# Sliding-window attention and token mixing on one core: heads on the two partition halves, products in quarter tiles, nine-token loads

## The chip, the core and the metric

The kernel runs on one core of a Trainium2 chip. The core has five engines with queues of their own: PE (TensorE) multiplies matrices and writes to the accumulators in PSUM (eight banks), DVE (VectorE) and ACT (ScalarE) read PSUM and write SBUF, POOL (GpSimd) here mostly issues the loads that turn float32 into float16 on the way, and SP (SyncE) issues the stores. Both memories have 128 partitions. The metric is device time in microseconds (us), lower is better.

## The reference

Eight batches of eight heads, 576 tokens, 64 features a head. Attention has a causal window of 128 tokens and a bias that falls with distance; its output, 512 features a token, goes through a token-mixing layer without a softmax. Inputs and output are float32. Cut to what matters:

```python
def _attn_ref(q, k, v):                      # (8, 8, 576, 64) each
    scores = scale * np.matmul(q, k.transpose(0, 1, 3, 2))
    rel = pos[:, None] - pos[None, :]
    slopes = 2.0 ** (-8.0 * (np.arange(H) + 1) / H)
    bias = slopes[:, None, None] * (-np.abs(rel))[None]
    mask = (rel >= 0) & (rel < 128)
    scores = np.where(mask, scores + bias[None], -1000000000.0)
    attn = softmax(scores)
    return np.matmul(attn, v)

def _moe_ref(x, w_q, w_k, w_out):            # x: (8, 576, 512)
    wq, wk = x @ w_q, x @ w_k                # (8, 576, 64)
    W_tok = scale * np.einsum('bsd,btd->bst', wq, wk)
    mixed = np.einsum('bst,btd->bsd', W_tok, x)
    return np.maximum(mixed, 0.0) @ w_out
```

## The kernel before

Everything is written out as some 770 small operations ("ops": one group of matmuls, one copy, one load). They are numbered as they are made, and the text `ORDER` lists them in the order in which they are emitted: the number, a letter for the engine (P, A, D, G for POOL, S for SP), for PE the PSUM bank, and sometimes `+n/b`, which puts n matmuls of zeros (`keep`, line 592) ahead of the op. Each engine works through its own ops strictly in this order and waits where one needs another's result. A few copies may go to ACT or DVE; `ORDER` says to which.

A batch goes through these steps. The names are those of the ops.

- Loads (line 239, on POOL): for batches 1 to 5 the first 512 tokens of q and k come in rows of two tokens (`ldqk`), the last 64 apart (`ldqkt`); batches 6 and 7 (`ONE`) come in rows of one token; batch 0 comes in rows of six tokens (`ldsix`), into the buffer that later takes outputs. v comes in rows of one token, one transfer for every 128 tokens (`ldv`).
- Transposes on PE through the identity matrix (`tsix` line 339, `tqk` lines 360 and 366, `tqkt` line 382), and copies out of PSUM by ACT or DVE (lines 220 and 222), which put q and k with features on the partitions: two heads on 128 partitions.
- Scores (`sc`, line 415): ten matmuls for a pair of heads and half of its keys. Each uses a quarter of PE's array, 64 rows by 64 columns; keys are on the partitions of the result. ACT takes the exponential (`exp`, line 420), 768 elements a partition in one instruction.
- Mask and bias as a table of factors `bt` (made at lines 251 to 268). For every pair of heads DVE multiplies twice: `edge` (line 435, 512 elements) writes the part of the window that crosses into the next block of 128 keys to a place of its own, and `mul` (line 439, 1,536 elements) treats the rest in place.
- Values (`pv`, line 459): 18 matmuls for a pair of heads, on the whole array (128 keys by 128 queries as weights), 65 columns each: 64 features and a column of ones that gives the softmax's sum. DVE takes the reciprocal (`rec`, line 472) and scales (`nrm`, line 475).
- Transposes of the result (`xt`, line 491) with a copy (`ext`), then the mixing: `wqk` (508), `wkt` (526), `g` (538), `mx` (554) with relu (`emx`, 561 and 563), and the output product `po` (575): four matmuls of 512 columns, a copy (`eo`), and a store (`st`, 582).

PE's matmuls come in five shapes (rows by columns of the array): 128x128 (`pv`, `xt`, `wqk`, `wkt`, `po`, `tqkt`, `tqk` of `ONE`, the zeros), 64x64 (`sc`), 128x64 (`tqk`, `g`), 64x128 (`mx`) and 96x64 (`tsix`). Going through `ORDER`, the shape changes 151 times. There are 2,362 matmuls, each with a weight load of its own, 43 of them of zeros.

Of the kernel before, what the change touches and what calls it, by code (L numbers as in the profile page):

```python
# [7 lines left out]
FP32 = mybir.dt.float32  # L8
F16 = mybir.dt.float16
# [4 lines left out]
P = 128  # L14
S = 576
# [11 lines left out]
0D 1D 32G 2G 28G 3D 22D 31G 4D 30G 29G 33G 137G 23D 6A 9A 53P7+13/7 35G 7A 11A 45P6 34G 134G 51P5+4/0 136G 52A  # L27
49P4 21G 50D 47P5+3/0 46D 133G 72P0 48A 74P2 55P4 132G 8A 5A 54A 40G 63P5+3/6 75A 59P7 39G 60D 12A 73A 36G 13D
61P2+3/2 16D 76D 43G 57P1+1/7 62A 56D 149P7 17G 64A 38G 147P0 85P2 58A 65D 135G 148D 18A 94P4 86A 150D 145P6
44G 95A 96P2+1/0 146D 83P0 97A 143P5+1/7 37G 10A 77D 42G 144A 14D 41G 78P2+1/4 84A 98D 228G 79D 186P6+3/4 80D  # L30
26G 87D 164P4+2/0 19D 99D 25G 151P3+1/0 165A 142G 66D 100P0 15A 152A 138G 88D 67P4 187A 188P2 139G 101D 68D
102D 189A 89P6 140G 69D 175P0 81P3 176A 141G 90D 166P4 91D 103P2 229G 104A 82D 92P7+2/0 190D 177P0 167A 153P2
232G 191D 178A 70P6+1/6 227G 24D 240P5+2/4 168D 71A 93D 231G 154A 179D 105P6+1/0 180D 321G 20A 241A 155P0 169D
230G 106A 107A 320G 108P5+1/2 170P2 109A 192P6 322G 156A 193D 244P5 194D 324G 110P4 181P0 171D 319G 172D 111A
245A 112P6 416G 182D 157D 114P2 238P4 115A 158D 242P5 323G 113A 118P2 239A 119D 159P6 234G 243D 195P3 160D
183D 270P4 246P2 235G 161D 116P0 247A 117D 173P7 336P6 419G 174D 271A 272P0 337D 184P2 273A 338P7 418G 196A
274D 248P0 250P4 237G 275D 332P6 249A 251A 339D 283P0 233G 162P3 281P4 163A 252D 333D 185A 236G 282A 334P7
197P2 27G 253D 284A 259P4 329G 335A 198D 330P6 260A 414G 285D 200P7 431P1 199A 201D 261P4 325G 331D 432A 202P7
417G 262A 203D 353P0 340P2 286D 415G 210P6 354A 351P4 211D 352A 326G 254P0 263D 341A 276P6 255D 327G 256D
364P4 362P2 264D 363A 287P0 365A 328G 277D 129P3 288D 278D 342P4 511G 289D 130A 375P6 257P2 343A 265P0 510G  # L40
126P3 344D 376A 258D 601G 429P5 345D 290P4 127A 208P6 291A 266D 433P3 507G 267D 209A 425P2 355D 279P4 434A
366D 268P7 509G 373P0 280D 430A 269D 204P3 426D 374A 516G 206P6 427P5 207A 292P0 605G 356D 428A 346P6 508G
205D 293A 123P5 347D 294A 506G 348D 295P4 448P2 377D 296A 705G 435P0 124D 449A 297P7 421G 436A 459P4 298D
357P2 367D 424G 460A 301P0 457P6 302A 358D 368P4 359D 458A 602G 446P0 369D 468P2 447A 370D 521P7 422G 349P6
469A 378D 305P0 470P4 423G 471A 212P3 461D 350D 306A 522D 437P4 420G 472D 299P6 303P0 438A 519P2 304D 213A
523P5 439D 706G 520A 517P4 462D 379P0 610G 518A 300D 120P3 606G 380D 524A 221P2 381D 697G 121D 371P7 222A
616P6 698G 450D 372A 382P5 617D 527P0 383A 609G 360P4 451D 538P2 361A 525P7 604G 440D 528A 384P4 514G 539A
526D 560P0 385A 607G 452P2 386D 387P7 215P6 561A 603G 453D 388A 562P4 454D 608G 216A 529P0 389P7 563A 473D
699G 716P6 530A 441P2 564D 512G 540P4 717D 551P0 390D 620P6 513G 442D 552A 224P7 621D 565D 541A 515G 463P0
225A 443D 391P4 700G 549P6 464D 392D 622P3 550A 702G 444P2 623D 618P5 445A 703G 397P6 465D 393P3 624P2 398A  # L50
619D 704G 395P0 394A 712P7 531D 396A 626P5 701G 625D 637P3 627A 474P0 532D 615G 307P2 638A 475D 713D 639P5
613G 308A 476D 714P4 640A 614G 533P2 715D 650P0 612G 542D 628P6 310P5 534D 629A 553D 543D 611G 466P4 651A
720P7 707G 535D 311A 218P6 709G 721A 630D 648P0 641D 544P2 631D 711G 649A 718P7 545D 219A 708G 566P0 546D 719A
455P5 567D 313P6 710G 467D 456A 568D 733P2 735P4 554D 632P0 736A 316P7 633D 314A 634D 555P4 734A 724P0 317A
556D 722P2 477P6 557D 725A 318S 217S 125S 399P7 131S 128S 220S 478D 723A 744P0 642D 661P4 659P2 745A 411P6
652D 737D 400A 726D 405P1 660A 653D 401S 547P7 662A 727D 643P2 412A 569P0 548D 406A 479P4 413S 226S 644D 570A
645D 536P7 480D 558P6 408P3 559D 481A 482P2 537D 755P0 409D 483A 746P4 757P6 756A 663D 410S 571P2 214S 315S
664D 747A 484P1 758A 572D 665P4 485D 573A 748D 574P7 646P6 666D 575A 488P0 667D 490P2 489A 576P7 486P4 491A
728P0 577D 487A 647D 492P2 582P6 729D 635P5 730D 583A 494P4 493A 759D 578P0 636D 584P6 580P2 760D 579A 497P5
581A 738D 654P0 585A 761P2 495A 655D 656D 739P6 498A 496S 223S 122S 309S 407S 500P4 749D 731P5 740D 668P1 762D  # L60
741D 732A 402P0 669D 750P6 763D 742P5 403A 657P1 751D 752D 586P3 404S 312S 658A 764P2 743A 753P7 765D 670P0
754D 587D 766P6 671D 589P5 672D 767A 673P3 769P2 590D 503P1 674D 592P5 501D 504A 770D 675P3 768A 505S 499S
502S 588S 591S 771P4 676A 593A 677P0 683P2 772D 595P7 678A 594S 684D 775P4 773P0 596D 679P2 598P6 776A 680D
597S 774A 681P4 779P2 599A 777P0 685P7 682D 778A 600S 780D 694P6 686A 784P5 687S 695D 691P4 696S 785D 790P7
786S 692D 793P6 693S 791D 688P5 792S 794D 787P4 795S 689A 781P7 690S 788D 789S 782A 783S
# [4 lines left out]
class Op:  # L70
    def __init__(self, name, engs, emit):
        self.name, self.engs, self.emit = name, engs, emit
        self.deps, self.ps_new, self.ps_read = set(), [], []
        self.eng = None
        self.pad = self.padbank = 0
# [11 lines left out]
class Plan:  # L87
# [5 lines left out]
    def op(self, name, engs, emit, reads=(), writes=(), ps_new=(), ps_read=()):  # L93
        o = Op(name, engs, emit)
# [21 lines left out]
    def run(self):  # L116
# [20 lines left out]
        assert len(order) == len(self.ops)  # L137
        return order


BOTH = ("ACT", "DVE")
FILL = ("ACT", "DVE", "POOL")
# [3 lines left out]
NPT = 6  # L146
# [5 lines left out]
ONE = (6, 7)  # L152
PTW = 64 + 4 * 256

VW = 80


@with_exitstack
def kernel(
# [16 lines left out]
    wone = pool.tile([P, P], F16, name="wone")  # L176
    rel = pool.tile([P, 256], I32, name="rel")
    wm = pool.tile([P, 256], FP32, name="wm")
    wtmp = pool.tile([P, 256], FP32, name="wtmp")

    bt = pool.tile([P, H, 512], F16, name="bt")
# [3 lines left out]
    nat = [[pool.tile([P, 2, 2 * DM], F16, name=f"nat{x}{i}") for i in range(NN)] for x in "qk"]  # L185
    ntl = [pool.tile([P, DM], F16, name=f"ntl{i}") for i in range(NN)]
    vn = [pool.tile([P, NT, H, VW], F16, name=f"vn{i}") for i in range(NV)]
    qkT = [pool.tile([P, 2, 4, S], F16, name=f"qkT{i}") for i in range(NQ)]


    pts = [pool.tile([P, 2, PTW], F16, name=f"pt{i}") for i in range(NPT)]
    inv = [pool.tile([P, 2, NT], FP32, name=f"inv{i}") for i in range(4)]
    xs = [pool.tile([P, NT, DM], F16, name=f"x{i}") for i in range(NX)]
# [10 lines left out]
    osh = osa.bitcast(F16)  # L204
    six = [osh[0:96, NOS - 6 + 3 * x : NOS - 3 + 3 * x].rearrange("p a n -> p (a n)").rearrange("p (h e) -> p h e", h=H)
           for x in range(2)]
# [17 lines left out]
    def fill(e, o, x):  # L224
        if e == "POOL":
            nc.gpsimd.memset(o, float(x))
        elif e == "DVE":
            nc.vector.memset(o, float(x))
        else:
            n = 1  # L230
            for y in o.shape[1:]:
                n *= y
            w = (wone if x else wz)[o.base_partition() : o.base_partition() + o.shape[0], 0:n]
            names = "abc"[: len(o.shape) - 1]
            k = dict(zip(names, o.shape[1:]))
            nc.scalar.copy(o, w.rearrange(f"t ({' '.join(names)}) -> t {' '.join(names)}", **k))
# [3 lines left out]

    def setup():
        plan.op("zero", ("DVE",), lambda e: nc.vector.memset(wz, 0.0), writes=["wz"])  # L242
        plan.op("one", ("DVE",), lambda e: nc.vector.memset(wone, 1.0), writes=["wone"])
        plan.op("iota", ("POOL",),
                lambda e: nc.gpsimd.iota(rel, pattern=[[1, 256]], base=0, channel_multiplier=-1),
                writes=["rel"])
        plan.op("idn", ("DVE",),
                lambda e: nc.vector.tensor_scalar(out=idn, in0=rel[:, 0:128], scalar1=0, scalar2=None,
                                                  op0=ALU.is_equal), reads=["rel"], writes=["idn"])
# [388 lines left out]
```

## Time and profile before

| | us |
|---|---|
| median of 3 runs | 148.21 |
| lowest and highest run | 147.70, 148.61 |
| span of the profiled execution, first to last instruction | 146.2 |
| PE busy in the span | 134.8 |
| DVE busy | 122.2 |
| ACT busy | 109.6 |
| POOL busy | 86.1 |

The span leaves out what lies before the first and after the last instruction. The profiled execution's whole time isn't listed apart; the median is 2.0 us above its span. The profile's page gives busy times, the span in 40 slices, the DMA queues and the chain of work that ended last. Its other views are groups of instructions by line and shape ("busy, mean ns of one | idle before"), a table by stages, a timeline in order of time, and the chain piece by piece. A busy PE isn't PE at its peak: matmuls are pipelined, and the recorded duration of one (379 ns for 512 columns) is longer than its turn. Turns are better read from the pieces of the chain, which follow without a gap.

### The profile page before, as it was taken

What the parts mean: (1) busy time and instruction counts of PE and PEld (TensorE: products, weight loads), DVE (VectorE), ACT (ScalarE), POOL (GpSimd) and SP (SyncE); (2) the same over time, 40 slices, a digit from 0 to 9 for tenths busy, and PEclk for the clock granted to TensorE, in tenths of its full rate; (3) what the DMA queues carried; (4) which work ended last, traced back from release to release, by engine and by line L of the source; (5) the groups of instructions that cost most, each with busy time, mean ns of one, the idle gap of its engine ahead of it and who ended that gap; (6) DMA issues with size and microseconds to landing.
All of it is one profiled execution on the core that took longest, in us unless ns stands there. A gap on an engine that the chain in (4) does not pass through costs nothing.

```text
span 146.2 us, 5403 instructions
## 1 busy us (share of the span) xinstructions
PE 134.8 (92%) x2319; PEld 87.9 (60%) x2319; DVE 122.2 (84%) x229; ACT 109.6 (75%) x172; POOL 86.1 (59%) x114
## 2 busy tenths in 40 slices
PE   6979889999898889999999999999989999999990
PEld 2444547667675566767667676676667577653430
DVE  3634899977999998999999999998989898868750
ACT  3329969897699987999999889899959872557121
POOL 6999999999578976898899999910000000000000
PEclk9999999999999999999999999999999999999997
DMA  2999999999999999999999999990957018329684
GB/s 28 135 171 178 162 142 140 132 162 179 178 173 159 178 178 164 166 169 173 154 153 137 149 152 155 136 128 12 378 193 281 8 59 300 147 97 376 259 321 172
DMA packets 90855, 24.59 MB, mean 168 GB/s; under 512 B 84176, under 2 KB 86224, under 8 KB 90832
## 3 DMA queue, kind: packets, MB, share of 16 engines
q0 software_dynamic: 85648, 14.82, 130.2%
q1 hardware_dynamic: 5184, 9.44, 17.4%
q8 instruction: 18, 0.29, 0.7%
q14 instruction: 5, 0.04, 0.1%
HBM read 29.62 MB, written 9.44 MB: 267 GB/s over the span
## 4 chain that ended last, share of the span: by engine, by line
PE 45%; ACT 20%; DVE 14%; DMA 10%; issue 6%; POOL 2%; SPq 1%; ACTq 0%; DVEq 0%; POOLq 0%
PE psb L575 15%; ACT pt L420 9%; PE psb L459 7%; DMA out_dram<-osa 6%; PE psb L415 5%; DMA osa<-in_k_dram 4%; DVE x L475 4%; PE psb L491 3%; ACT qkT L220 3%; ACT rm L561 3%; PE psb L360 3%; PE psb L366 3%; ACT xT L220 2%; PE psb L554 2%; PE psb L508 2%
## 5 line engine op out<-in xcount | busy, mean ns | idle before, releaser
L420 ACT ACTIVATE pt<-psb 128x768 f16<-128x768 f32 x64 | 49.8, 819 | 6.2 <-PE psb L415 5.2
L239 POOL DMA_DIRECT2D vn<-in_v_dram x44 | 36.6, 887 | 3.6 <-DMA natq<-in_q_dram 2.4
L575 PE MATMUL psb<-wout,rm 128*128 128x512 f16 x144 | 35.2, 379 | 0.2
L439 DVE TENSOR_TENSOR pt<-pt,bt 128x1536 f16<-128x1536 f16 x32 | 29.9, 949 | 0.2
L475 DVE TENSOR_TENSOR x<-psb,inv 128x640 f16<-128x640 f32 x32 | 26.0, 820 | 0.7
L459 PE MATMUL psb<-vn,pt 128*128 128x65 f16 x576 | 22.4, 193 | 1.6 <-DVE pt L439 0.5
L222 DVE COPY qkT<-psb 128x1024 f16<-128x1024 f16 (+2 forms) x23 | 18.7, 822 | 5.6 <-PE psb L339 5.1
L459 PEld LDWEIGHTS <-pt 128*128 128x128 f16 x576 | 20.1, 97 | 5.0 <-issue 1.2
L220 ACT COPY osa<-psb 128x512 f32<-128x512 f32 x23 | 13.3, 590 | 12.3 <-PE psb L575 6.9
L220 ACT COPY qkT<-psb 128x1024 f16<-128x1024 f16 (+2 forms) x20 | 17.8, 912 | 4.2 <-PE psb L339 2.9
L415 PE MATMUL psb<-qkT 64*64 64x192 f16 (+2 forms) x640 | 20.1, 234 | 0.9 <-ACT qkT L220 0.4
L575 PEld LDWEIGHTS <-rm 128*128 128x128 f16 x144 | 12.7, 98 | 12.7 <-issue 1.1
L415 PEld LDWEIGHTS <-qkT 64*64 64x64 f16 x640 | 11.6, 106 | 9.7 <-issue 7.0
L239 POOL DMA_DIRECT2D natk<-in_k_dram x18 | 16.2, 938 | 1.7 <-DMA natk<-in_k_dram 1.2
L239 POOL DMA_DIRECT2D natq<-in_q_dram x18 | 16.8, 938 | 0.0
L592 PE MATMUL psb<-wz 128*128 128x512 f16 x43 | 13.8, 427 | 1.5 <-DVE wz L242 1.3
L491 PE MATMUL psb<-idn,x 128*128 128x128 f16 x160 | 13.6, 219 | 0.9 <-ACT osa L220 0.5
L435 DVE TENSOR_TENSOR pt<-pt,bt 128x512 f16<-128x512 f16 x32 | 12.9, 414 | 1.2 <-ACT pt L420 1.0
L561 ACT ACTIVATE rm<-psb 128x576 f16<-128x576 f32 x21 | 12.8, 653 | 1.5 <-PE psb L554 1.0
L491 PEld LDWEIGHTS <-x 128*128 128x128 f16 x160 | 10.0, 98 | 3.9 <-issue 1.1
L222 DVE COPY osa<-psb 128x512 f32<-128x512 f32 x13 | 9.0, 689 | 2.7 <-PE psb L575 2.3
L220 ACT COPY xT<-psb 128x576 f16<-128x576 f16 x15 | 9.4, 647 | 1.8 <-PE psb L491 1.8
(62 smaller groups left out, 162.2 us busy)
## 6 DMA issues: line engine op xcount, KB each, us to landing
out_dram<-osa SPq DMA_DIRECT2D x36, 256.0 KB, 2.9
vn<-in_v_dram POOLq DMA_DIRECT2D x28, 128.0 KB, 4.9
natq<-in_q_dram POOLq DMA_DIRECT2D x10, 256.0 KB, 6.8
natk<-in_k_dram POOLq DMA_DIRECT2D x10, 256.0 KB, 7.2
vn<-in_v_dram POOLq DMA_DIRECT2D x16, 64.0 KB, 4.8
natq<-in_q_dram POOLq DMA_DIRECT2D x8, 128.0 KB, 5.2
natk<-in_k_dram POOLq DMA_DIRECT2D x8, 128.0 KB, 5.1
osa<-in_q_dram POOLq DMA_DIRECT2D x4, 144.0 KB, 4.1
```

Source lines behind the costliest of these rows:

```text
L220: nc.scalar.copy(o, i)
L222: nc.vector.tensor_copy(out=o, in_=i)
L239: plan.op(name, ("POOL",), lambda e: nc.gpsimd.dma_start(out=dst, in_=src), reads=reads, writes=writes)
L415: nc.tensor.matmul(ps32(g)[half : half + 64, o : o + w], T[r, 1, hp, k0 : k0 + 64], T[r, 0, hp, q0 : q0 + w], start=True, stop=True)
L420: nc.scalar.activation(out=blocks(pt)[:, :, 2 * u : 2 * u + 2, 0:192], in_=ps32(g).rearrange("t (a c) -> t a c", a=2)[:, :, 0:384].rearran ...
L439: nc.vector.tensor_tensor(out=o, in0=o, in1=bt[:, 2 * hp : 2 * hp + 2, 0:192].unsqueeze(2).broadcast_to([P, 2, 4, 192]), op=ALU.mult)
L459: nc.tensor.matmul(ps32(g)[:, o : o + D + 1], pt[:, a, c : c + 128], vv[:, kb, 2 * hp + a, 0 : D + 1], **flags)
L475: nc.vector.tensor_tensor(out=xb[:, :, 128 * hp : 128 * hp + 128].rearrange("t j (a d) -> t a j d", a=2), in0=px()[:, :, :, 0:D], in1=iv.u ...
L491: nc.tensor.transpose(ps16(g)[:, 128 * t : 128 * t + 128], xb[:, t, 128 * hp : 128 * hp + 128], idn)
L561: nc.scalar.activation(out=o, in_=s, func=AF.Relu, scale=WSCALE)
L575: nc.tensor.matmul(ps32(g), rm[p % NR][:, db, o : o + 128], wout[:, db, :], start=(db == 0), stop=(db == 3))
L592: nc.tensor.matmul(psb[:, b, :], wz[:, 0:P], wz[:, 0:DM], start=True, stop=True)
```

## The change

Attention is laid out anew. Before, two neighbouring heads shared an op and all 128 keys of a block lay on the partitions. Now an op holds four heads: two of the first four heads of the batch on partitions 0 to 63 and two of the last four on 64 to 127, and keys come in blocks of 64, nine to a head.

- Scores: an op has four quarter matmuls for each of two (the last: three) key blocks, in all 576 instead of 640. A block of 64 keys sees 192 queries in one stretch, so nothing crosses into another block. `edge` goes, and `mul` treats two key-block halves of four heads with 1,536 elements; 32 of them stay.
- Values: 50 quarter matmuls (64 keys by 64 queries, 65 columns) take the place of 18 whole ones, 1,600 instead of 576. `xs` and the weights' rows change their order of features to match.
- `mx` is cut into quarters as well (four matmuls, not two). `po`, `xt`, `wqk` and `wkt` can be emitted whole ("F") or as two halves of 64 columns ("H"). The new `shapes` picks, for PE's order as it is, the forms with the fewest changes. With this order it picks "H" everywhere, so that PE knows two shapes, quarters (Q) and halves (H), beside the zeros; the shape changes 104 times. There are 3,802 matmuls, 26 of them of zeros.
- q and k come in rows of nine tokens, one transfer for all heads of a batch; q goes to partitions 0 to 63 and k to 64 to 127 of one tile, so that a transpose turns both. v comes in four transfers a batch. In all POOL issues 56 transfers instead of 105.
- Batch 0: heads 0, 1, 4 and 5 are loaded as float32 by SP and cast by DVE (`cast`, twice 1,152 elements). The other four heads come first on POOL, ahead of the count (`iota`) from which the identity matrix and the table are made; before, `iota` came behind one transfer.
- The table is made by four exponentials of 768 elements instead of eight of 256. The fills of ones and zeros shrink. `pt` has four buffers of four heads, before six of two.
- A new order, with other shares: of the 32 `ext` DVE has 26 (before 17), of `emx` 9 (11), of `eo` 14 (13), of the copies of 1,024 elements after `tqk` 13 (14, and 4 of 576); ACT has the rest. The first stores come about halfway through the order; before, they came after the last load. After the last `pv` PE has still to do `wkt`, `po`, `g`, three `xt`, two `mx`, `xt`, `po`, two `mx`, `wqk`, two `po`, `wkt`, `po`, `g`, `po`, three `mx`, `po`, `mx` and five `po`.

```diff
 ORDER = """
+0D 12D 11D 9D 10D 26G 25G 27G 28G 1G 113G 112G 31G 16G 32G 30G 29G 199G 198G 13G 14G 15G 117G 114G 115G 116G 17G 18G
+23S 22S 20S 19S 2D 3D 6A 5A 7A 39P0+13/7 40D 24D 41P1+1/2 42D 43P0 44A 4A 8D 35P2 36D 21D 67P0+2/3 68A 71P4 72A 65P6
...
+    def shapes(self, pe):
+        cost, path = {None: 0}, {None: ()}
+        for o in pe:
+            best = {}
+            for f in o.forms:
+                was = min(cost, key=lambda p: cost[p] + (p != f) + (1 if o.pad and "F" not in (p, f) else 0))
+                best[f] = (cost[was] + (was != f), (path[was], f))
...
-NPT = 6
+NPT = 4
...
+    def wide(f, o, w, x, **flags):
+        if f == "F":
+            nc.tensor.matmul(o, w, x, **flags)
+            return
+        for a in range(2):
+            r = slice(64 * a, 64 * a + 64)
+            nc.tensor.matmul(o[r], w[:, r], x, **flags)
...
+            for i in range(2):
                 for x, src in ((0, q), (1, k)):
+                    def ldf(e, i=i, x=x, src=src):
+                        nc.sync.dma_start(out=raw[64 * x : 64 * x + 64, i],
+                                          in_=src[0, 4 * i : 4 * i + 2].rearrange("h (p j) d -> p h (j d)", j=9))
...
+                    cp(e, nat[0][:, 4 * i : 4 * i + 2, :], raw[:, i])
...
+                load("ldqk0" if b == 0 else "ldqk", nat[n][64 * x : 64 * x + 64, h, :],
+                     src[b, h].rearrange("h (p j) d -> p h (j d)", j=9),
+                     [("nat", n, x, y) for y in (range(4) if ys is None else (ys,))])
...
+                load("ldv", vn[n][64 * c : 64 * c + 64, 2 * u : 2 * u + 2, :, 0:D].rearrange("p g t d -> p (g t) d"),
+                     v[b, h : h + 2].rearrange("g (t p) d -> p (g t) d", p=D), [("vn", n, u, c)])
...
+                    kbs = range(2 * u, 2 * u + 2 if u < 3 else 9)
+                    for kb in kbs:
+                        w = min(192, S - 64 * kb)
+                        o = at(kb) - 384 * u
+                        for c in range(2):
+                            for r in range(2):
+                                i, y = slice(64 * r, 64 * r + 64), 2 * c + Q
+                                nc.tensor.matmul(ps32(g)[64 * c : 64 * c + 64, 512 * r + o : 512 * r + o + w],
+                                                 T[i, 1, y, 64 * kb : 64 * kb + 64], T[i, 0, y, 64 * kb : 64 * kb + w],
+                                                 start=not added, stop=not added or kb == kbs[-1])
...
-            def edge(e, pt=pt, hp=hp):
-                w = bt[:, 2 * hp : 2 * hp + 2].rearrange("t a (k c) -> t a k c", c=128)[:, :, :, 64:128]
-                s = blocks(pt)[:, :, :, 0:64]
-                d = pt[:, :, 0:1024].rearrange("t a (k c) -> t a k c", k=4)[:, :, :, 0:64]
-                nc.vector.tensor_tensor(out=d, in0=s, in1=w, op=ALU.mult)
...
-        def pv(e, g=g):
-            for a in range(2):
-                def mm(t, c, kb, **flags):
-                    o = 512 * a + (D + 1) * t
-                    nc.tensor.matmul(ps32(g)[:, o : o + D + 1], pt[:, a, c : c + 128], vv[:, kb, 2 * hp + a, 0 : D + 1], **flags)
...
+        def pv(f, g=g):
+            for t in range(NT):
+                ks = [[x for x in range(2 * t + e - 2, 2 * t + e + 1) if 0 <= x < 9] if 2 * t + e < 9 else [8] for e in range(2)]
+                for i in range(3):
+                    for e in range(2):
+                        if i >= len(ks[e]):
+                            continue
+                        kb = ks[e][i]
+                        a = at(kb) + 64 * (min(2 * t + e, 8) - kb)
+                        for c in range(2):
+                            s = slice(64 * c, 64 * c + 64)
+                            o = 512 * c + (D + 1) * t
+                            nc.tensor.matmul(ps32(g)[64 * e : 64 * e + 64, o : o + D + 1], pt[s, r, a : a + 64],
+                                             vv[s, hp, kb, 0 : D + 1], start=(i == 0), stop=(i == len(ks[e]) - 1))
```

More of the change, by code (lines that the diff above doesn't have):

```diff
@@ L150 @@
 NOS = 14
-ONE = (6, 7)
-PTW = 64 + 4 * 256
+ADD = ()
+PW = 1536
 VW = 80
+FAR = 1.0e9
+LOW = -60000.0
 @with_exitstack
@@ L224, in fill @@
     def fill(e, o, x):
[L225 to L236, printed above, removed]
+        (nc.gpsimd if e == "POOL" else nc.vector).memset(o, float(x))
@@ L241, in setup, with iota @@
     def setup():
         plan.op("zero", ("DVE",), lambda e: nc.vector.memset(wz, 0.0), writes=["wz"])
[L243 to L249, printed above, removed]
+        def iota(e):
+            for a in range(2):
+                nc.gpsimd.iota(rel[64 * a : 64 * a + 64], pattern=[[1, 192]], base=0, channel_multiplier=-1)
@@ L251, in dist, with unit @@
+        def unit(e):
+            nc.vector.memset(idn, 0.0)
+            for a in range(2):
+                r = slice(64 * a, 64 * a + 64)
+                nc.vector.tensor_scalar(out=idn[r, r], in0=rel[r, 0:64], scalar1=0, scalar2=None, op0=ALU.is_equal)
+        plan.op("iota", ("POOL",), iota, writes=["rel"])
+        plan.op("idn", ("DVE",), unit, reads=["rel"], writes=["idn"])
         def dist(e):
@@ new lines, in setup, with table, copies @@
+        if len(ADD) < NB * 4:
+            for g in range(4):
+                def table(e, g=g):
+                    nc.scalar.activation(out=bt[:, g].rearrange("t (k c) -> t k c", c=192),
+                                         in_=wms.unsqueeze(1).broadcast_to([P, 4, 192]),
+                                         func=AF.Exp, scale=-(2.0 ** -(g + 1)))
+                plan.op("table", ("ACT",), table, reads=["wms"], writes=[("bt", g)])
+            def copies(e):
+                nc.vector.tensor_copy(out=bt[:, :, 704:768], in_=bt[:, :, 0:64])
+            plan.op("copies", ("DVE",), copies, reads=[("bt", g) for g in range(4)], writes=["be"])
@@ L605 @@
                 keep(o.padbank, o.pad)
-            o.emit(o.eng)
+            o.emit(o.form if o.eng == "PE" else o.eng)
     return plan
```

424 lines of the change are left out of this document (188 added, 236 removed).

## The prediction

> **What bounds the kernel now.** I read the page first, then the table of stages, then the chain piece by piece. By the page no engine holds the chain alone:
>
> ```profile
> PE 45%; ACT 20%; DVE 14%; DMA 10%; issue 6%; POOL 2%; SPq 1%; ACTq 0%; DVEq 0%; POOLq 0%
> ```
>
> So the span is cut in three: the start, the stretch up to the last `pv`, and the end. Columns are length, then busy time of PE, PE's weight loads, DVE, ACT and POOL.
>
> ```profile
> 0.00:20.00 20.00, 16.80 (x267) 8.86 (x268) 11.84 (x29) 12.49 (x23) 18.29 (x33) 1.00 1.36 136
> 20.00:122.40 102.40, 98.28 (x1915) 68.89 (x1912) 95.92 (x179) 88.11 (x134) 67.84 (x83) 1.00 1.70 158
> 122.40:146.20 23.80, 19.67 (x149) 10.17 (x145) 14.48 (x24) 9.03 (x16) 0.00 (x0) 0.97 0.64 239
> ```
>
> The middle is bound twice: PE is busy 98.3 of 102.4 us and DVE 95.9. Work taken from one of them alone would leave the other. DVE is idle for 8.2 us in the start and 6.5 us in the middle. The end belongs to PE. The granted clock is full (1.00) in the first two stages. The chain shows what a turn of PE costs, since its pieces follow one another without a gap:
>
> ```profile
> 77.31 0.57 PE psb L366 x16
> 77.87 1.09 PE psb L508 x8
> ...
> 79.25 0.65 PE psb L459 x18
> 80.05 0.86 PE psb L575 x4
> ...
> 81.37 0.67 PE psb L538 x10
> ...
> 82.36 0.55 PE psb L459 x18
> ...
> 92.67 0.97 PE psb L575 x4
> ```
>
> The same 18 matmuls of `pv` take 0.55 us behind a group of their own shape and 0.65 behind another shape; the four of `po` take 0.86 or 0.97. A change of shape thus costs 0.10 us, and 151 of them some 15 us. A matmul of 512 columns has a turn of 0.215 us (0.42 ns a column), and one `pv` matmul of 65 columns 0.55/18 = 0.031 us.
>
> **The change, part by part.**
>
> *Changes of shape.* 151 become 104: PE saves 47 x 0.10 = 4.7 us. The price is that `po`, `xt`, `wqk` and `wkt` go as halves, two matmuls for one. Line 366 is such a pair: 16 matmuls of 128 columns in 0.57, less 0.10 for the change. That is 0.059 us for each two, while 128 columns alone need 0.054: the halves run side by side. I count them at nothing; one after the other they would double `po` (36 x 0.86 = 31 us), which that row excludes.
>
> *Values.* The 50 quarter matmuls of a `pv` are spread over the four quarters, 13 on the fullest. If the quarters run at once at `pv`'s present turn, that is 13 x 0.031 = 0.40 us instead of 0.55: 32 x 0.15 = 4.8 us saved. If they don't, the nearest rows are the scores, the only quarters there are:
>
> ```profile
> 17.50 0.53 PE L415 MATMUL psb<-qkT 64*64 64x64 f16 x20
> ...
> 76.95 0.36 PE L415 MATMUL psb<-qkT 64*64 64x64 f16 x10
> ```
>
> Ten more matmuls add 0.17 us, 17 ns each. At 17 ns, 50 would take 0.85 us and PE would lose 9.6 us. But in those ten each quarter streams 384 columns, which alone take 384 x 0.42 = 0.16 us: the row shows columns as the limit and doesn't show how fast short matmuls can be issued. I take 0.40 and keep 0.85 as the upper end; with the pipeline's tail (0.53 for 20, 26 ns each) it would be 1.3 us. [...]
>
> *`edge` and the other work of DVE.* Groups by line and shape, then two of DVE's copies of 1,024 elements in the timeline, then `edge` on the chain:
>
> ```profile
> L222 DVE COPY qkT<-psb 128x1024 f16<-128x1024 f16 x14 | 13.7, 986 | 0.3
> ...
> L435 DVE TENSOR_TENSOR pt<-pt,bt 128x512 f16<-128x512 f16 x32 | 12.9, 414 | 1.2 <-ACT pt L420 1.0
> ...
> L222 DVE COPY xT<-psb 128x576 f16<-128x576 f16 x17 | 7.4, 448 | 1.1 <-PE psb L491 0.9
> ...
> L222 DVE COPY qkT<-psb 128x576 f16<-128x576 f16 x4 | 2.9, 754 | 5.1 <-PE psb L339 5.1
> ```
>
> ```profile
> 60.72 1.22 DVE L222 COPY qkT<-psb 128x1024 f16<-128x1024 f16 x1
> ...
> 86.47 0.69 DVE L222 COPY qkT<-psb 128x1024 f16<-128x1024 f16 x1
> ```
>
> ```profile
> 110.11 0.34 DVE pt L435
> ```
>
> `edge` lasts 0.414 us but fills 0.34 on the chain; 32 of them free 10.9 us. `mul` keeps its 32 instructions of 1,536 elements. Against that: nine more `ext`, 9 x 7.4/17 = 3.9 us. The copies behind `tqk` become 13, all with a stride, so at 1.22 us (0.69 is the contiguous form of the batches of single tokens, which goes): 15.9 us, where 14 copies (0.986 on the mean) and batch 0's four of 576 strided elements (0.754) took 16.8; 0.9 us less. The two casts of 1,152 elements have no row; by the rows of 576 elements, doubled, they take 0.9 us (contiguous) to 1.5 (strided), and I take 1.0 each, since they are contiguous: 2.0 more. Fills, table and the other exchanged copies come to an estimated 2 us less, between 0 and 4. DVE sheds 10.9 + 0.9 + 2 - 3.9 - 2.0 = 8 us: 122.2 becomes 114. ACT gives up nine `ext` and takes other copies; at 109.6 us and idle for a quarter of the span it bounds nothing, and gets no term.
>
> *The start.* These rows stand in the timeline:
>
> ```profile
> 2.17 0.37 POOL L245 IOTA rel<- 128x256 int32 x1
> ...
> 5.63 1.34 ACT L261 ACTIVATE bt<-wm 128x256 f16<-128x256 f32 x4 [3.61 <-DVE wm L256]
> ...
> 12.20 0.82 ACT L420 ACTIVATE pt<-psb 128x768 f16<-128x768 f32 x1
> ```
>
> And the first issues of q (shortest, median and longest in ns, first and last start):
>
> ```profile
> L239 POOL DMA_DIRECT2D osa<-in_q_dram x4: 672/677/766, 1.3 to 6.9; - x4
> ```
>
> POOL now issues four loads before `iota`, not one; at 0.68 us each `iota`, cut in two, ends near 5 us instead of 2.5. Behind it wait the identity matrix, so every transpose, and the five short steps to the table: ACT's exponentials move from 5.6 to about 8 us and, four at some 0.8, last to 11. DVE has two copies and a cast in that time, and the first `exp` needs both; it comes at about 12 us as before. Two of the next batch's wide loads stand on POOL's queue ahead of the first v, which the first `pv` waits for. I leave DVE's idle start at 8 us, bounds 6 to 11. The 17 matmuls of zeros that go lie where PE waits and count nothing.
>
> *Loads.* The bytes stay the same:
>
> ```profile
> HBM read 29.62 MB, written 9.44 MB: 267 GB/s over the span
> ```
>
> POOL issues half as often. Its waits bound nothing now, so I count nothing; the cover is that from batch 3 on q and k are issued, counted in DVE's instructions of the new order, over 20 us of work before their transposes. The stores that now start halfway share the DMA with the loads: 0 in the sum, up to 3 us if a batch comes late. That ACT no longer waits for stores in the end gains little, since PE is what ends it.
>
> *The end.* Now from the last `pv` (122.4) to PE's last matmul 20 us pass, then a copy and a store:
>
> ```profile
> 133.97 0.47 PE psb L554 x6
> 134.44 7.89 PE psb L575 x36
> ...
> 142.36 0.58 ACT osa L220
> ```
>
> From 142.3 to the span's end are 3.9 us, and they stay. In the new order PE has after the last `pv` twelve `po` (10.3), four `xt` (1.1, five turns of 0.056 each), eight `mx` (1.0), a `wqk` (1.0), two `g` (1.1), two `wkt` (0.3) and nine changes (0.9): 15.7 us, and 0.5 for waits. DVE has some 9 us there, where it had 14.5.
>
> **The sum.** Up to the last `pv` DVE must do 114 - 9 = 105 us, before 107.8: most of what it sheds, it pays back by taking work out of the end. With 8 us idle in the start and 5 in the middle (before 6.5; PE, with 4.8 us less of `pv` and most of the 4.7, no longer holds it up) the last `pv` comes at 118.3 instead of 122.4. Then 16.2 and 3.9: a span of 138.4. With the 2.1 us around the span (148.2 less 146.2) that is 140.5 us.
>
> **The rivals.**
>
> *Slower: the quarter matmuls of `pv` take turns.* One mechanism: each short quarter costs PE a turn of its own, whatever its quarter. For it speaks that every row of quarters fits 17 ns a turn or more; against it that those rows are filled by columns. At 26 ns a `pv` takes 1.3 us and PE's middle gets 98.3 - 4 + 32 x 0.75 = 118 us (4 of the 4.7 for changes lie there); with 4 idle the last `pv` comes at 142 and the end at 164 us. At 17 ns (0.85 us) PE's middle is 104, the last `pv` 128 and the time 150. It breaks even with today's 148.2 at about 0.79 us a `pv`, 16 ns a matmul. Chance 0.17 for slower than that by 1% or more.
>
> *In between: PE's queue is filled too slowly.* PE has 2 x 3,802 = 7,604 instructions where it had 4,724; over 138 us that is one every 18 ns. In the middle stage now, 3,827 in 102.4 us are one every 27 ns. Nothing shows a faster steady supply. At one in 6 to 8 ns within a `pv` (0.6 to 0.8 us) PE loses 6 to 13 us of what I forecast, the middle is bound by PE, and by the same sum the time is 142 to 148.5. [...] Chance 0.16.
>
> *Loads late.* Wide rows are no faster by the byte and batch 1 comes before v of batch 0: 2 to 4 us are lost in the start or when stores begin, 142.5 to 144.5. Chance 0.09.
>
> *Better than forecast.* DVE's idle time in the middle all but goes once PE has slack, and the start gains 2 us: 135 to 137. Chance 0.06.
>
> **How the numbers follow.** The forecast has 0.52, its own range is 137 to 143 (`pv` up to 0.5 us, the start and the small copies at their bounds). A measurement of this kernel tells about 1% from no change: the three runs differ by 0.6%. Faster by over 1% (below 146.7) are the forecast, the better case, the late loads and two thirds of the slow supply: 0.52 + 0.06 + 0.09 + 0.10 = 0.77. Within 1% is the rest of the slow supply, 0.07 with a little of the slower case; slower 0.16. The range 135 to 148.5 leaves out the slower case and little else.
>
> **What would show it.** Right: `edge`'s line is gone, a `pv` of 50 fills 0.40 to 0.45 us on the chain, a change still costs 0.10, the groups of `po` stay at 0.86 as halves, DVE is busy about 114 us, the last `pv` starts near 118 us and PE ends 16 us later. Wrong: a `pv` over 0.6 us, PE idle with "issue" inside a group, transposes that wait for a DMA after 20 us, or DVE still at 120 us.

## The result and the profile after

| | before | after |
|---|---|---|
| median of 4 runs, us | 148.13 | 183.12 |
| lowest and highest | 147.70, 148.61 | 181.68, 184.53 |
| span of the profiled execution | 146.2 | 180.6 |

The ratio is 1.233, with a 95% interval of 1.225 to 1.240: the kernel is 23% slower, outside the predicted range on the side that had 0.16. (The ratio leaves out the run of 184.53 us as a slow one: its granted clock was 0.891, where the other three had 0.896 to 0.905.) These lines of the page of after have the busy times, PE and its granted clock in 40 slices, the queue that brings instructions, and the chain by engine:

```profile
PE 139.1 (77%) x3802; PEld 96.5 (53%) x3802; DVE 120.5 (67%) x195; ACT 119.3 (66%) x162; POOL 44.1 (24%) x62
...
PE   7669684973587987298837799789697998679992
...
PEclk9969969999769999889995579978999999978999
...
q8 instruction: 29, 0.48, 1.1%
...
PE 53%; issue 17%; ACT 14%; DVE 8%; DMA 4%; POOL 1%; DVEq 0%; POOLq 0%
```

No engine is full any more. PE, which was busy 92% of the span, is busy 77%, and 17% of the chain is "issue", time in which PE waited for nothing that the profile shows. The clock, which before was full but for the last slice, sinks to 5 to 7 tenths in several slices. The groups of PE with the most idle time ahead of them say the same; the last columns are the idle time and what ended it:

```profile
L470 PE MATMUL psb<-vn,pt 64*64 64x65 f16 x1600 | 21.9, 203 | 15.0 <-issue 15.0
...
L470 PEld LDWEIGHTS <-pt 64*64 64x64 f16 x1600 | 19.3, 115 | 19.0 <-issue 18.1
```

The chain of after piece by piece (start, length, what) shows where that time lies:

```profile
70.76 0.45 PE psb L470 x47
71.21 0.30 PE psb L422 x8
71.51 0.40 PE psb L261 x10
71.91 0.14 PE psb L470
72.06 3.49 issue
75.55 0.92 PE psb L470 x43
...
90.57 0.40 PE psb L370 x10
90.97 3.13 issue
94.10 0.36 PE psb L370 x6
94.46 0.29 PE psb L422 x8
94.75 0.41 PE psb L470 x47
```

At full clock a `pv` that no stop disturbs takes 0.41 to 0.45 us behind quarters, as forecast. Behind another shape it fills 0.54 or 0.55 on the chain, the 0.10 of a change more; one of these eight longer ones stands behind quarters all the same. But now and then PE stops for some 3 us in the middle of a group, here once inside a `pv` and once inside a group of transposes (L370), and the `pv` behind the first stop runs at half pace (0.92; the granted clock is 0.50 from 75.0 to 78.4 us). The kind of instruction doesn't matter. What the stops have in common is their place in PE's sequence. PE's records (weight loads, matmuls, and the 21 waits and drains of its queue) were numbered in order of time, and for every 256th, counted from the 192nd, the time from its start to the start of the next record was taken. The table has twelve of these times, worked out from the trace:

| record | 960 | 1216 | 1472 | 1728 | 1984 | 2240 | 2496 | 2752 | 3008 | 3264 | 3520 | 3776 |
|---|---|---|---|---|---|---|---|---|---|---|---|---|
| us to the next | 2.91 | 1.35 | 2.55 | 3.13 | 1.73 | 0.02 | 0.01 | 3.69 | 0.00 | 0.12 | 3.35 | 2.76 |

In the whole execution 14 of these pauses are over 0.3 us and come to 28.9 us; without the record's own time, some 0.2 to 0.4 us each, PE is idle for 25.3 us in 13 of them. In before the same count gives one pause, of 0.37 us, with 0.29 us of PE idle, first for ACT and then for 0.15 us of issue. The page of before has the row that goes with it:

```profile
q8 instruction: 18, 0.29, 0.7%
```

18 packets with 0.29 MB, 16 KB each, for 2 x 2,319 instructions of PE are one packet for 256 instructions; after, 29 packets for 2 x 3,802. (Of before the text above counts 2,362 matmuls; the page's 2,319 hold the zeros already.) By these counts PE gets its instructions by DMA in blocks of 256, and stops where the next block isn't there. The times of these packets in the trace say the same: there is one for every edge of a block, and each of the 14 pauses ends 1.3 to 1.8 us after a packet has landed. Counting a pause to the block behind it, before spends 88.3 us on 13 blocks (31.2 to 119.5 us), 6.8 us each. After spends 81.4 us on the same 13 (29.0 to 110.4), 6.3 each, while loads run, and 45.9 us on the next 11, 4.2 each, when the loads are almost over.

One other thing is new. The copies after the transposes of q and k, on ACT (L235) and DVE (L237), by line and shape:

```profile
L235 ACT COPY qkT<-psb 128x1024 f16<-128x1024 f16 x19 | 19.7, 1069 | 1.2 <-DVE pt L445 0.8 <-PE psb L370 0.3
...
L237 DVE COPY qkT<-psb 128x1024 f16<-128x1024 f16 x13 | 15.9, 1235 | 7.2 <-PE psb L370 7.1
...
L235 ACT COPY qkT<-psb 128x512 f16<-128x512 f16 x5 | 12.3, 2464 | 0.0
...
L237 DVE COPY qkT<-psb 128x512 f16<-128x512 f16 x2 | 4.9, 2444 | 0.0
```

The copies of the ninth token, half as long as the others, take twice as long: 2.45 us for 512 elements.

### The profile page after: what moved, and what is told of

It reads as the page before. It is cut to its first block, busy times and chain, and to the rows that moved or that the text cites. A ratio compares the mean times of both kernels' runs of the same rounds, so it can differ in the third digit from the quotient of the medians.

```text
span 180.6 us, 8301 instructions
## 1 busy us (share of the span) xinstructions
PE 139.1 (77%) x3802; PEld 96.5 (53%) x3802; DVE 120.5 (67%) x195; ACT 119.3 (66%) x162; POOL 44.1 (24%) x62
## 4 chain that ended last, share of the span: by engine, by line
PE 53%; issue 17%; ACT 14%; DVE 8%; DMA 4%; POOL 1%; DVEq 0%; POOLq 0%
PE psb L253 19%; PE psb L470 9%; PE psb L422 7%; ACT qkT L235 7%; PE psb L261 6%; PE psb L370 6%; ACT pt L427 6%; DMA nat<-in_k_dram 4%; DVE qkT L237 4%; PE psb L561 3%; PE psb L543 2%; POOL nat L243 1%; DVE x L481 1%; DVE osa L237 1%; DVE pt L445 1%
## 5 line engine op out<-in xcount | busy, mean ns | idle before, releaser
L253 PE MATMUL psb<-wout,rm 128*64 128x512 f16 x288 | 38.8, 397 | 3.0 <-ACT qkT L235 1.6
L235 ACT COPY qkT<-psb 128x1024 f16<-128x1024 f16 (+2 forms) x25 | 32.0, 1357 | 3.8 <-PE psb L370 2.9
L470 PE MATMUL psb<-vn,pt 64*64 64x65 f16 x1600 | 21.9, 203 | 15.0 <-issue 15.0
L470 PEld LDWEIGHTS <-pt 64*64 64x64 f16 x1600 | 19.3, 115 | 19.0 <-issue 18.1
L370 PE MATMUL psb<-idn,nat 128*64 128x128 f16 x576 | 23.7, 237 | 6.6 <-issue 3.5
L237 DVE COPY qkT<-psb 128x1024 f16<-128x1024 f16 (+2 forms) x16 | 21.6, 1389 | 7.2 <-PE psb L370 7.1
L370 PEld LDWEIGHTS <-nat 128*64 128x64 f16 x576 | 20.4, 121 | 10.6 <-issue 8.7
L253 PEld LDWEIGHTS <-rm 128*64 128x64 f16 x288 | 15.6, 113 | 14.9 <-issue 5.9
L235 ACT COPY osa<-psb 128x512 f32<-128x512 f32 x22 | 13.0, 593 | 8.5 <-PE psb L253 8.3
L261 PE MATMUL psb<-idn,x 128*64 128x128 f16 x320 | 16.9, 255 | 1.7 <-issue 1.7
L237 DVE COPY xT<-psb 128x576 f16<-128x576 f16 x26 | 11.5, 454 | 7.9 <-PE psb L261 7.6
L261 PEld LDWEIGHTS <-x 128*64 128x64 f16 x320 | 13.1, 132 | 5.0 <-issue 3.6
L237 DVE COPY osa<-psb 128x512 f32<-128x512 f32 x14 | 9.5, 687 | 7.2 <-PE psb L253 7.2
```

The costliest lines, as they stand in the source:

```text
L235: nc.scalar.copy(o, i)
L237: nc.vector.tensor_copy(out=o, in_=i)
L253: nc.tensor.matmul(o[r], w[:, r], x, **flags)
L261: nc.tensor.transpose(o[r], w[:, r], i)
L370: nc.tensor.transpose(o[64 * a : 64 * a + 64], w[:, y, a, j, :], idn)
L470: nc.tensor.matmul(ps32(g)[64 * e : 64 * e + 64, o : o + D + 1], pt[s, r, a : a + 64], vv[s, hp, kb, 0 : D + 1], start=(i == 0), stop=(i = ...
```

## The experiments

The theory: PE's instructions come in blocks of 256, one after the other, and the blocks come no faster than one in about 4 us, or 6 beside the loads; the change needs 11 blocks more in less time. Rivals: short quarter matmuls cost more turns than forecast; late loads; the long copies; DVE.

**The supply by itself.** A kernel with nothing but 3,200 quarter matmuls of 65 columns in one stretch, alone and then beside all loads of q, k and v. The reference isn't computed.

```python
for i in range(3200):
    e, c = i // 2 % 2, i % 2
    s = slice(64 * c, 64 * c + 64)
    nc.tensor.matmul(psb[64 * e : 64 * e + 64, c, 0:65], wz[s, 0:64], wz[s, 64:129], start=True, stop=True)
```

> The kernel does nothing but 3,200 quarter matmuls of 65 columns on constants, four quarters in turn, with a weight load each, and no loads: 6,400 instructions, 25 blocks of 256. Fetch theory (PE's instructions come in blocks of 256, and a block takes 3.5 us or more to arrive): the stream takes 25 x 3.5 = 85 to 90 us, with a gap at every 256th instruction and 30 ns for four matmuls between the gaps. Theory that short quarters take turns: no gaps, an even 16 ns or more a matmul, 51 us or more. Neither: 800 x 0.03 = 24 us.

> The same stream beside the loads of all eight batches in the changed kernel's form (rows of nine tokens for q and k, of one for v). Fetch theory: blocks share the DMA engines with the loads, so while the loads last (some 80 to 90 us) a block takes about 6 us, then 3.5: 120 us or more for the stream. Turn theory: as without loads, within a few per cent.

98.7 and 129.6 us. The chain of the first (parts of it), then its row of the clock:

```profile
6.29 1.24 PE psb L38 x128
7.53 2.76 issue
...
42.64 2.03 issue
44.67 1.98 PE psb L38 x107
46.64 2.03 issue
48.67 1.97 PE psb L38 x120
50.64 1.48 issue
52.12 1.97 PE psb L38 x111
```

```profile
PEclk9996555555555555555555555555555555555555
```

And the chain of the second, while the loads run:

```profile
36.07 4.22 issue
40.29 1.98 PE psb L38 x97
42.27 4.22 issue
46.49 1.97 PE psb L38 x117
48.46 4.50 issue
```

A block of 128 matmuls and their weight loads takes 1.98 us, then PE has nothing to do for 1.5 to 2.0 us, or for some 4.2 beside the loads: a block in 3.45 to 4.0 us (3.76 on the mean, somewhat more than expected), or in 6.2 (5.9 to 6.75). These are close to the 4.2 and 6.3 of after. Nothing but the loads on the DMA differs between the two, and their end shows in the second kernel: from about 82 us on its blocks come in 3.45 to 4 us again. The packets' times show where a block's time goes. Alone, the next packet (but for the last one) starts 1.0 to 1.7 us after PE has gone past an edge, lasts 0.9 to 1.4, and PE goes on 1.2 to 1.6 after its end. Beside the loads the packet itself takes no longer (0.9 to 1.0), but starts only after 3.6 to 4.3 us. PE works at half clock from about 8 us on (0.541 on the mean of the span), while it pauses at every block. But the half clock doesn't set the pace: the block from 6.29 us on, ahead of that, took 1.24 us, and PE then waited for 2.76 instead of 2.0.

**After with fewer loads, and with fewer instructions.** The loads of batches 3 to 7 left out (those batches compute on old data), and then a `pv` with 20 matmuls instead of 50 (each query block sees its own key block alone).

```diff
-                for i in range(3):
+                for i in range(1):
...
-                        kb = ks[e][i]
+                        kb = ks[e][-1]
```

> The changed kernel without the loads of batches 3 to 7 (their heads are computed from the older contents of the buffers). Fetch theory: the blocks of the middle arrive in 3.5 to 4 us instead of 6, the stalls of 2.5 to 3.7 us shrink to under 1.5 us, time 155 to 168 us. Theory that late loads hold the transposes: the waits for loads go as well, but the gaps at every 256th instruction don't change; 172 to 180 us. Turn theory: no change, 180 to 184 us.

> The changed kernel with 20 instead of 50 matmuls in every pv (each block of queries is multiplied with its own block of keys alone): 960 matmuls and 1,920 PE instructions fewer, 7.5 blocks. Fetch theory: 7.5 blocks at some 4 to 5 us that could not be hidden, 145 to 158 us. If only PE's time in pv counted: 32 x 0.25 = 8 us less, 173 to 177 us.

164.4 and 155.1 us, against 183.1. The pauses over 0.3 us at the blocks' edges fall from 28.9 us to 14.0 and to 9.3. Without the loads PE has every instruction that it had, and is 19 us faster. In the second, `pv` has 30 of its 50 matmuls less, at 0.41 to 0.45 us a `pv` some 8 us of PE's turns, and 28 us come off. Both fit blocks; the rival of late loads expected 172 to 180 us for the first, with the same gaps, and the rival that a short matmul's turn is the cost 173 to 177 for the second.

**The same on the kernel before.** Each `po` matmul of 512 columns as eight of 64, nothing else.

```diff
-                for db in range(4):
-                    nc.tensor.matmul(ps32(g), rm[p % NR][:, db, o : o + 128], wout[:, db, :],
-                                     start=(db == 0), stop=(db == 3))
+                for z in range(0, DM, DM // 8):
+                    for db in range(4):
+                        nc.tensor.matmul(ps32(g)[:, z : z + DM // 8], rm[p % NR][:, db, o : o + 128],
+                                         wout[:, db, z : z + DM // 8], start=(db == 0), stop=(db == 3))
```

> The kernel before, with each of the four 512-column matmuls of a po group written as eight of 64 columns, same shape, same order, same place: 1,008 matmuls more, so PE has 6,740 instructions instead of 4,724 (27 blocks of 256 instead of 19). Columns, bytes and changes of shape stay. Theory (PE's instructions come in blocks of 256, one per 3.5 to 4 us without loads and about 6 us beside them): the kernel before is just inside that supply with a block per some 6.5 us, and this takes it over: PE stops with the reason issue at every 256th instruction, 64 short of the multiple, for 0.5 to 3 us each, 153 to 165 us in all. Rival (a matmul costs only its turn on PE, so many instructions alone harm nothing): the same columns and some 3 us of added turns, 148 to 151.5 us, no stops at every 256th instruction.

155.4 us, against 147.8. (By the page's count it has 2 x 3,327 instructions.) Its groups keep their turns, and the stops are there, five of them at the blocks' edges with 4.9 us; one in the chain:

```profile
74.13 0.17 PE psb L366
74.31 1.11 issue
75.42 1.53 PE psb L366 x47
...
77.61 1.84 PE psb L576 x63
```

63 slices take 1.84 us where two groups of four, at 0.86 each, took 1.72, so the columns and the turns cost nearly what they did: 0.06 us more a group, some 2.2 us for all 36. With the stops that is most of the 7.6. The stop stands inside the transposes behind a `po`, not in `po`: the group that spends the instructions isn't the one that waits. The time lies at the lower end of what the theory gave, since only `po` spends more.

**The ninth token.** Tokens 7 and 8 are transposed and copied together, in runs of two, in two copies (q, k) instead of one; the long copies take tokens 0 to 6.

```diff
-                turned("tqk", (y,), range(8), Ps(1))
+                turned("tqk", (y,), range(7), Ps(1))
...
-                turned("tqkt", (0, 1, 2, 3), (8,), Ps(1))
+                turned("tqkt", (0, 1, 2, 3), (7, 8), Ps(1))
```

> The kernel after, with the ninth token's copies made in runs of two elements: tqk transposes tokens 0 to 6, the tail operation tokens 7 and 8, copied once for q and once for k. The number of transposes, the shapes and the order stay. If the 2.45 us of a 512-element tail copy come from writing single two-byte elements, each of the two new copies of 512 pairs-wise written elements takes 1.3 us or less, and the seven long ones fall from 2.45 to about 2 x 1.2 us or less; if they come from the distance between writes, each takes over 2 us. On the time: by the theory that PE's instruction supply holds the kernel, at most 4 us change, 179 to 184 us; by the rival that the long copies on ACT and DVE hold it, 7 x 1 to 1.5 us come off, 173 to 177 us.

180.5 us. The copies of tokens 7 and 8:

```profile
L235 ACT COPY qkT<-psb 128x512 f16<-128x512 f16 x10 | 10.5, 1178 | 0.0
L237 DVE COPY qkT<-psb 128x512 f16<-128x512 f16 x4 | 4.1, 1120 | 0.6 <-PE psb L370 0.6
```

512 elements in runs of two take 1.15 us, where as single elements they took 2.45. The long copies were a cost of the change that the prediction didn't have, but at most some 2.7 us of the time hang on them (one run; those of after lie up to 2.9 us apart). The stops stay, 28.4 us, and so the rival that those copies hold the kernel falls.

**The layout with fewer instructions.** A `pv` in 36 matmuls instead of 50 (14 of them with 128 queries, which two query blocks share), whole matmuls again for `po`, `wqk`, `wkt`, most `xt`, and `mx` in two where that costs no change of shape; the ninth token as above. PE has 2 x 2,902 instructions. Then the same without the loads of batches 3 to 7 (old data as before).

```diff
+                for part in f:
+                    for t in range(NT):
+                        if part == "R":
+                            todo = [(0, kb) for kb in (2 * t - 1, 2 * t) if 0 <= kb and t < 4]
+                        else:
+                            todo = [(0, 2 * t - 2)] if t else []
+                            todo += [(1, 2 * t + 1)] if t < 4 else [(1, 8), (0, 7), (0, 8)]
+                        for e, kb in todo:
+                            w = 128 if part == "R" else 64
```

> The kernel after with the same layout and order but fewer PE instructions, some 5,806 instead of 7,606: a pv as 14 matmuls of 64 keys by 128 queries and 22 quarters (36 instead of 50), po, wqk, wkt, xt and mx as whole matmuls where halving does not save a change of shape, and the ninth token in runs of two as in after_pairs. Changes of shape rise from 104 to about 179, 7.5 us at 0.10. By the theory of instruction blocks, seven blocks fewer at 3.5 to 6 us each come to 25 to 40 us less on the supply, of which PE's own work takes back 7.5 and more: 148 to 162 us, with fewer and shorter stops at every 256th instruction. By the rival that the turns of PE are the cost, the added changes make it slower than after: 185 us or more.

> after_lean with the loads of q, k and v of batches 3 to 7 left out (those batches compute on old data), so that instruction blocks come in 3.5 to 4 us instead of some 6 while few other transfers run. after_lean has 12 us of stops at every 256th instruction and waits for loads besides. By the theory of instruction blocks nearly all stops behind the first loads go, and the time is 147 to 154 us; that would be about the time before, so that the change without its instruction bound would have gained nothing either. If the stops do not come from the supply, it stays above 159 us; if the prediction's sum had been right but for the supply, it would come to 141 to 146 us.

163.9 us, 19 less than after although the shape changes 75 times more often, but 1.9 above what was expected: 12.1 us of stops are left, all ahead of 110 us, where loads run. Without the loads it is 152.6, with 2.2 us of stops, as expected. So even when its instructions come nearly in time, this lean form isn't faster than before; the likely reason, which no run takes apart, is that it has given back the halves and quarters that saved turns. Whether the full form would be, with a faster supply, no run can show.

**What held the kernel before.** The prediction had let DVE's 8 us bring the last `pv` forward. `edge` left out after its first use on each buffer; `pv` with 12 matmuls instead of 18; both. The later heads' values are off in all three.

```diff
-                nc.vector.tensor_tensor(out=d, in0=s, in1=w, op=ALU.mult)
+                if 4 * b + hp < NPT:
+                    nc.vector.tensor_tensor(out=d, in0=s, in1=w, op=ALU.mult)
...
-                    mm(t + 1, c + 128, t, start=False, stop=(t == 3))
+                    if t == 3:
+                        mm(4, c + 128, 3, start=False, stop=True)
```

> The kernel before without edge after its first use on each buffer (the masking of the edge columns is left out from then on, so the values of the later heads are off): DVE loses some 26 x 0.414 = 10.8 us, nothing else changes. If DVE's work alone sets half of the middle, as the prediction's sum had it, the last pv comes some 3 to 8 us earlier: 140 to 145.5 us. If PE alone holds the middle (98.3 of 102.4 us busy), the gain is under 2 us: 146.3 to 148.3.

> The kernel before with 12 instead of 18 matmuls in a pv (the contribution of the key tile ahead is left out for query tiles 1 to 3): PE loses 32 x 6 x 0.031 = 6.0 us and 384 instructions, DVE nothing. If PE alone holds the kernel from about 60 us on (its row there is 98 to 100% busy) the part of it behind 60 us, some 3 us, comes off and the late loads hold the rest: 144 to 146 us. If DVE holds the middle as much as PE, as the prediction had it, nothing or little comes off: 146.5 to 148.

> Both at once: 12 matmuls in a pv as in before_short_pv, and edge left out after its first use on each buffer. PE loses 6.0 us, DVE 10.8. If the middle is bound by PE and DVE both, as the prediction's sum had it, the two together bring the 6 us and more that neither brings alone: 140 to 143 us. If PE and the loads hold it, the time is that of before_short_pv within 1 us.

Without `edge` 147.7 us against 147.8, ratio 0.9995 (0.996 to 1.003): nothing. With the short `pv` 145.0 (two runs) against 147.95, ratio 0.980 (0.974 to 0.986); with both 144.8 (two runs), ratio 0.978 (0.972 to 0.984). Two stages of before, then of before without `edge` (columns as above):

```profile
20.00:60.00 40.00, 36.78 (x786) 26.34 (x782) 36.58 (x70) 33.60 (x50) 34.02 (x43) 1.00 1.97 162
60.00:120.00 60.00, 59.10 (x1099) 40.90 (x1097) 56.94 (x105) 53.87 (x84) 33.82 (x41) 1.00 1.57 151
```

```profile
20.00:60.00 40.00, 36.45 (x783) 26.00 (x781) 33.62 (x60) 33.78 (x51) 32.76 (x41) 1.00 1.89 157
60.00:120.00 60.00, 59.02 (x1105) 40.97 (x1103) 51.44 (x87) 53.97 (x84) 35.24 (x42) 1.00 1.63 155
```

From 60 us on PE is busy 59.1 of 60 us; taking 5.5 us off DVE there leaves PE's column as it was. Ahead of 60 us PE has idle time, and there the chain of the kernel without `edge` runs over loads:

```profile
35.38 9.57 DMA natq<-in_q_dram
...
49.35 9.36 DMA natk<-in_k_dram
```

So before is bound by PE alone from 60 us on, and ahead of that loads take DVE's place as soon as DVE has less to do. DVE was 94% busy in the middle and still gave nothing.

**A version that gains.** The kernel before in its own order and layout, `mx` in quarters and `xt`, `wqk`, `wkt` as halves only where that saves a change of shape, for 57 matmuls more.

```diff
+        kinds = dict(tsix="S", tqk="H", tqk1="F", tqkt="F", sc="Q", pv="F", xt="FH", wqk="FH", wkt="FH", g="H", mx="RQ", po="F")
```

> The kernel before in its own order and layout, with mx in quarters and xt, wqk and wkt as halves where that saves a change of shape: about 14 changes fewer, 1.4 us at 0.10 each, for 57 matmuls and 114 instructions more (4,754 instead of 4,640). By the readings of this case PE holds the second half, so 0.7 to 1.4 us come off: 146.4 to 147.4 us. If changes of shape were not the cost that the chain shows, or if DVE held the middle, the time stays within 0.3 us; the rival that any added instruction costs supply time has it up to 1 us slower.

147.23 us (12 runs) against 147.95 (17 runs), ratio 0.9948 (0.9925 to 0.9971): half a per cent faster than before. It is the best of the versions that compute the whole reference, at the lower end of what the 14 changes of shape that it saves promised.

## Why the prediction was wrong

- **Supply of instructions: the step that failed.** The sum has no term for it. The prediction put it among the rivals, at 0.16, and priced it as a slower pace inside a `pv` (6 to 8 ns an instruction, 6 to 13 us). It isn't a pace but a block: 256 instructions in 6.2 us beside loads, 24 ns each on the mean, and 3.45 to 4.0 us without. Within a block PE takes them faster than that rival's 6 to 8 ns: the 100 of a `pv` in 0.41 us, 4 ns each. The rate that the rival gave for before, one instruction every 27 ns, was already near that limit, and the 18 ns that the forecast needed were not to be had while loads run. (In before PE reaches three edges only 1.4 to 1.5 us after the packet has landed, no later than PE goes on in the stream: there it is at the limit already.) The stops leave PE idle for 25.3 us, and stretches at half clock, six of the eight behind the stops, cost it some 15 more (below): by this estimate 40 of the 42.6 us between forecast and measurement. The stops are a sign that the prediction had named itself, PE idle with "issue" inside a group. The size of the blocks could be worked out from the packets of q8 on the page of before, which the prediction didn't read. Whether a block is there in time goes by how long the one ahead of it keeps PE: before, at 6.8 us a block, has one pause over 0.3 us at 18 edges; the streams, whose blocks take PE 1.98 us, stop 24 times in 6,400 instructions.
- **Values, 0.40 us: right.** 0.41 to 0.45 us undisturbed and behind quarters. The rival of quarters that take turns, the predicted slower case, had the right sign by the wrong mechanism: luck.
- **Changes of shape, and halves at nothing: right.** Eight halves of `po` take 0.86 us behind their own shape and 0.98 behind another, as the chain's end shows:

```profile
158.95 0.48 PE psb L470 x34
...
169.96 0.86 PE psb L253 x8
...
171.31 0.98 PE psb L253 x8
...
172.54 4.46 PE psb L253 x40
```

- **PE's work: right, at full clock.** 134.8 us less 4.8 and 4.7 make 125.3. The 139.1 of after, times its mean clock of 0.905, are 125.9, and the 131.3 of the run with few loads, at 0.958, are 125.8. These are estimates, since the mean clock covers idle time too. Stretch by stretch, 29.8 us of PE's busy time in after lie where the clock was granted by half; counting them half leaves 124.2, and 124.5 for the run with few loads. The other 13 to 15 us that PE is busy came for the most part with the stops: behind them it runs slower, as the 0.92 for a `pv` (0.41 to 0.45 at full clock) and the stream's 0.541 show.
- **DVE, 8 us: wrong twice.** DVE shed 1.7 us, not 8 (122.2 to 120.5): `edge` went and the copies of 1,024 took 1.235 us as forecast, but the small copies, put at 2 us less, brought the ninth token's 2.45 us each, 4.9 on DVE and 12.3 on ACT, which got "no term" and rose by 9.7. And what DVE shed could not have paid: without `edge` before stays at 147.7. The sum took the last `pv` forward by DVE's load, where PE alone and the loads set it; for PE's 9.5 us the run with the short `pv` shows the rate, 2.9 us for 6.0 taken off.
- **The start: late.** The first `exp` comes at 14.2 us instead of about 12. Against 35 us this is small.
- **The end: 16.2 us, near.** From the last `pv` (its end at 159.4, in the rows above) to PE's last matmul (177.0) are 17.6 us; the granted clock of that stage is 0.90.
- **Loads, nothing: wrong in another way than the rival had it.** On the chain of after a DMA stands once, up to 10.8 us, and then no more, so late loads aren't the cause. But while loads run a block of instructions takes 6.2 us instead of 3.45 to 4.0 (the streams), and POOL, which waits for the slowed PE, ends its last issue at 120.4 us, where it was 95.6 before.

## What to carry to other kernels

Before cutting matmuls into quarters to save turns, divide the time that PE would need by its instructions (two for each matmul with weights of its own): here less than some 24 ns an instruction beside loads, or 14 to 16 without, was not to be had, and the instruction queue's packets on the page tell how near a kernel is. Stops at every 256th instruction, at any line, with "issue" as the reason, are the sign; the group that stands in front of them need not be the one that spends the instructions. DVE, busy for 95.9 of 102.4 us in the middle of before (94%), was no bound: without `edge` the time stayed at 147.7 us against 147.8. So the chain should be asked which engine's pieces follow without a gap.

## What the hardware showed that was not expected

- Instruction blocks come one at a time and with a latency: in the stream alone, with 0 tenths in every slice of the page's DMA row, the packet of 16 KB takes 0.9 to 1.4 us on its queue, yet a block comes every 3.45 to 4.0 us. The rest lies ahead of the packet (1.0 to 1.7 us after PE has passed the edge) and behind it (1.2 to 1.6 us until PE goes on). Loads lengthen the wait ahead of the packet, to 3.6 to 4.3 us, and not the packet; why isn't shown by any run here.
- PE's granted clock was 0.50 from 20 to 60 us of the stream alone, where PE stops for 1.5 to 2.0 us in every 3.45 to 4.0, and in after it was 0.50 within 1.5 us of the end of six of the seven stops over 2 us. What lowers it, no run here takes apart.
- Copies from PSUM that write single two-byte elements 18 bytes apart take 4.8 ns an element on ACT and DVE alike (2,464 and 2,444 ns for 512); in runs of two 2.2 to 2.3 (1,178 and 1,120 ns), in runs of eight 1.04 and 1.21 (1,069 and 1,235 ns for 1,024).
